# Moving every SBUF buffer of a fused attention and two-layer feed-forward kernel to a fixed place modulo 256 bytes

## The chip, the cores and the metric

The kernel runs on one core of one Trainium2 chip. The metric is the device time of one execution in microseconds, as a median over runs; beside it there is one execution taken with the hardware profiler, and all rows of a trace in this document come from such an execution. Every value is 32 bits wide, a tile has 128 partitions, and an address in this text is a byte offset within one partition of SBUF.

## The reference

Three blocks follow each other. The first is attention with random features, per batch (4) and head (8), sequence 576, head width 64, 128 features:

```python
q_p, k_p = phi(q * scale), phi(k * scale)    # phi: exp(x @ omega.T - |x|^2 / 2 - max) / sqrt(m)
kv = einsum('bhsm,bhsd->bhmd', k_p, v)
num = einsum('bhsm,bhmd->bhsd', q_p, kv)
den = einsum('bhsm,bhm->bhs', q_p, k_p.sum(axis=2)) + 1e-06
x = (num / den).transpose(0, 2, 1, 3).reshape(2304, 512)
```

The second (layer 1) is `(silu(x @ w_gate) * (x @ w_val)) @ w_out` with 1536 hidden columns, the third (layer 2) is `g(x @ w_in) @ w_out` with 2048 hidden columns, where `g` is 0 below -1, `(h + 1)^2 / 4` between -1 and 1, and `h` above 1.

## The kernel before, in words

**Order.** A planner in Python runs the whole kernel as a set of processes with priorities and a cost for each step, and thereby writes out by hand one fixed order of instructions for each engine. On the chip the engines run those orders and wait for each other through semaphores. A wait that ends late on the chip does not change the order.

**Products.** Nearly all work of TensorE is in `split3` (lines 398 to 400). Each operand is kept as a high and a low part in fp32r, and a product of two operands is three matmuls, high by high, high by low, low by high, each with a stationary operand of 128 columns and a moving operand of 256 columns:

```python
nc.tensor.matmul(ps, l_hi, r_hi, ...)   # L398: (accumulator, stationary, moving)
nc.tensor.matmul(ps, l_hi, r_lo, ...)   # L399
nc.tensor.matmul(ps, l_lo, r_hi, ...)   # L400
```

Each matmul has its own weight load, and the load for the next matmul runs while the present one streams. So the pair of addresses that are read together is the home of the next stationary operand and the home of the present moving operand.

**Stages.** Until about 257 us attention is computed, with the first part of layer 1 between its products. From 257 to about 601 us the rest of layer 1 follows, from there to the end layer 2. The late stages go through passes over four sets of weights in each layer (`passes`), in each over blocks of 512 tokens, with seven products for a 2 by 2 split of the block (`SEVEN`, `set_up`). In the order of TensorE the up products (x times the first weights) alternate with the down products (hidden rows times the second weights).

**Roles.** In the up products and in the down products of layer 1 (`out1`, `down1`) the weights are stationary, and what streams is x or the hidden row. In the down products of layer 2 (`down2`, `down_end`) the roles are turned: the hidden row is stationary and the weights stream. In attention the stationary operands are `ki`, `qi`, `ebk`, `ebq`, `xhl`, `kvz`, the moving ones `omr`, `omh`, `oml`, `vi`, `ids`, `qt`.

**Homes.** A ring is a list of free buffers of one role. The weights' slots are the rings' tiles `w` (9), `wx` (7, on the space of `lent` once attention's first block is done) and `wb` (8, on the space of `att` after attention, in the pool `rb`); x lives in `x1s` and `xur`, hidden rows in `hl` and `hlr`. Pools hand out addresses in the order of the code. The first 1,152 bytes are taken, so `pad0` of 352 bytes puts `w` at 1,504 + 4,096 i, which is 224 modulo 256; `pad1` of 160 puts `x1s` at 50,848, which is 160. With the other pads all of `w`, `wx`, `wb` are at 224 and all of `x1s`, `xur`, `hl`, `hlr` at 160. In attention `ebk`, `ebq`, `ki`, `vi`, `qi` and `xhl` are at 64, `qt`, `kvz` and `ids` at 192, `omr`, `omh`, `oml` at 224.

Of the kernel before, what the change touches and what calls it, by code (L numbers as in the profile page):

```python
# [42 lines left out]
SLACK_D, SLACK_U = 3.0, 0.8  # L43

SLACK_A = 0.0

NATK = 3

# [232 lines left out]
def performer_moe_kernel(ctx: ExitStack, tc: tile.TileContext, qG, kG, om, ident,  # L281
# [10 lines left out]
    def ring(*a):  # L292
        return Ring(bufs(*a))
# [4 lines left out]
    keep = ctx.enter_context(tc.tile_pool(name="keep", bufs=1, side="left"))  # L298
    acc = []
    bank = ring(psum, "bank", 8, [P, 512])  # L300
    def pad(pool, name, nbytes):
        pool.tile([P, nbytes // 4], F32, name=name)

    pad(keep, "pad0", 352)
    wring = ring(keep, "w", 9, [P, 2, 512], F32R)
    wstage = ring(keep, "ws", N_WS, [P, 1024], U32)
    wtmp = ring(keep, "wt", 2, [P, 512])
    half = keep.tile([P, 1], F32, name="half")
# [4 lines left out]
    x2q = [[dram.tile([P, KD, 512], F32, name=f"x2q{a}_{b}") for b in range(NBLK // 2 + 1)] for a in range(len(SETS1) - 1)]  # L313
    x2d = [dram.tile([P, 2, NBLK * TB], F32, name=f"x2d{d}") for d in range(2)]

    pad(keep, "pad1", 160)
    x1_sets = ring(keep, "x1s", 3, [P, 2, KD, TB], F32R)
    hbuf = ring(keep, "hb", 3, [P, 512])
    hrow = ring(keep, "hl", 2, [P, 2, 512], F32R)
    osb = ring(keep, "os", 3, [P, 512])  # L320
    xin = ring(keep, "xi", 2, [P, 512])
    xpart = ring(keep, "xp", 2, [P, 512])

    att_cm = tc.tile_pool(name="att", bufs=1, side="right", reuse_waits="tile")
    att = att_cm.__enter__()
    ebufs = {False: ring(att, "ebk", EBK, [P, 512]), True: ring(att, "ebq", EBQ, [P, 512])}
    kin = ring(att, "ki", KINS, [P, 512])
    vin = ring(att, "vi", VINS, [P, 576])
    qin = ring(att, "qi", QINS, [P, 512])
    lent_cm = tc.tile_pool(name="lent", bufs=1, side="left", reuse_waits="tile")  # L330
    lent = lent_cm.__enter__()
    lent_ids = set()
# [19 lines left out]
    lend(vin, "vl", N_VL, [P, 576])  # L352
    lend(qin, "ql", 2, [P, 512])
    lend(ebufs[False], "el", 2, [P, 512])
    nat_b = sorted({b for b in range(4) for k in range(NATK) if b * 576 < (k + 1) * TB and k * TB < (b + 1) * 576})
    kvr = {(b, d): att.tile([P, 2, 2, P], F32, name=f"kvr{b}_{d}") for b in nat_b for d in range(2)}
    qts0 = ring(att, "qtn", 3, [P, 2, TB])
    xhl = ring(att, "xhl", 2, [P, 2, 256], F32R)
    stat = ring(att, "st", 10, [P, 4, 4])
    rec = ring(att, "rec", 2, [P, TB])  # L360
    qts = ring(att, "qt", N_QT, [P, 2, 2, TB], F32R)
    kvz = [[att.tile([P, 2, 2, 2, P], F32R, name=f"kvz{b}_{d}") for d in range(2)] for b in range(2)]
    ids = att.tile([P, P], F32, name="ids")
    rect = ring(att, "rect", 1, [P, TB // 32, 33])
    nc.gpsimd.memset(rect.free[0][0][:, :, 32:33], 1e-6)
    omr = att.tile([P, 256], F32, name="omr")
    omh = att.tile([P, 256], F32R, name="omh")
    oml = att.tile([P, 256], F32R, name="oml")


    def dma(dst, src, nbytes):
# [52 lines left out]
        pl.put(wstage, st)  # L424
        return t

    def conv_key(key, src, slot):
        st = yield Get(wstage)
        pl.set(wdone[key])
        t = yield from to_f32(st, src, None)  # L430
        yield from parts(slot[:, 0], slot[:, 1], t, 512)
        pl.put(wtmp, t)
        wslot[key] = slot
        pl.set(wready[key])

    def conv(key, src, rng, prio):
# [2 lines left out]
        pl.spawn(conv_key(key, src, slot), prio)  # L439
        yield wdone[key]  # L440

    def wfree(key, rng):
        pl.put(rng, wslot.pop(key))

    moe_on = Ev()
    NE = N_EARLY[0]
# [55 lines left out]
    def w_feed():  # L502
        for m, a, order, sets in passes:
            for c in sets:
                for s, p in columns(m, c):
                    slots, tt = [], []
                    for i in range(2):
                        yield staged[s, 2 * p + i]
                    for _ in range(2):
                        tt.append((yield Get(wt2)))  # L510
                    for _ in range(4):
                        slots.append((yield Get(wring)))
                    pl.spawn(conv_pair(s, p, tt, slots), PR_W)
                for key in set_keys(m, c)[4:]:
                    yield staged[key]
                    t = yield Get(wt2)
                    slot = yield Get(wring)
                    pl.spawn(conv_one(key, t, slot), PR_W)

    def late_rank():  # L520
        return PR_C if moe_on.done else PR_CS
# [3 lines left out]
        wslot[key] = slot  # L525
        pl.set(wready[key])

    def conv_one(key, t, slot):
        yield from dma(t, w32[key], 262144)
        yield from conv_slot(key, t, slot)  # L530
        pl.put(wt2, t)

    def conv_pair(s, p, tt, slots):

        hs = [pl.spawn(dma(tt[i], w32[s, 2 * p + i], 262144), 0.6) for i in range(2)]
        for h in hs:
            yield h
        t0, t1 = tt
        lo, hi = slice(0, 256), slice(256, 512)
        yield from conv_slot((s, 2 * p), t0, slots[0])  # L540
        yield from conv_slot((s, 2 * p + 1), t1, slots[1])
        yield from two(t1[:, hi], t1[:, lo], t1[:, hi], 256, ALU.add)
        yield from two(t1[:, lo], t0[:, lo], t1[:, lo], 256, ALU.subtract)
        yield from two(t0[:, lo], t1[:, hi], t0[:, lo], 256, ALU.subtract)
        yield from two(t0[:, hi], t0[:, hi], t0[:, lo], 256, ALU.subtract)
        yield from conv_slot(("c" + s, p), t1, slots[2])
        pl.put(wt2, t1)
        yield from conv_slot(("d" + s, p), t0, slots[3])
        pl.put(wt2, t0)


# [376 lines left out]
    def att_close():  # L928
        for k in range(NBLK):
            yield x1_ready[k]  # L930
        att_cm.__exit__(None, None, None)
        rb = ctx.enter_context(tc.tile_pool(name="rb", bufs=1, side="right", reuse_waits="tile"))
        for rng, name, n, c in ((xpart, "xr", N_XR, [P, 512]), (ebr, "eb", N_EB, [P, 512]), (gbr, "gb", N_GB, [P, 1024]),
                                (wt2, "wtr", N_WT, [P, 512]), (hbuf, "hbr", N_HB, [P, 512]), (xq, "xq", N_XI, [P, 512])):
            for t in bufs(rb, name, n, c):
                pl.put(rng, t)
        for rng, name, n, more in ((hrow, "hlr", N_HL, 320), (wring, "wb", NB1, 192)):
            for t in bufs(rb, name, n, [P, 2, 512], F32R):
                pl.put(rng, t)
            pad(rb, "pad" + name, more)  # L940
        for t in bufs(rb, "xur", N_XU, [P, 2, 2, TB], F32R):
            pl.put(xu, t)
        pad(rb, "pad5", 320)
        pl.set(right_b)
        LEAN["DVE"], LEAN["POOL"] = LEAN_B, POOL_B

# [44 lines left out]
    def row_out(row, h):  # L991
        if len(row) > 2:
            if row[2] is not None:
                yield row[2]
        hl = yield Get(hrow)
        if len(row) > 2:
            pl.set(row[3])
        yield from parts(hl[:, 0], hl[:, 1], h, 512)
        pl.put(hbuf, h)
        row[1].append(hl)  # L1000
        pl.set(row[0])

    def evac1(k, d, last):
# [76 lines left out]
    def out1(step, h_ev, res):  # L1080
        k, fp = step
        first, last, end = run[step]
        for i in range(2):
            yield wready["o", 2 * fp + i]
        yield h_ev
        ws = [wslot["o", 2 * fp + i] for i in range(2)]
        hl = res[0]
        for n in range(KD):
            d, c = divmod(n, 2)
            if first and c == 0:  # L1090
                yield acc_free[d]
                acc_free[d] = Ev()
            for i in range(2):
                yield Op("PE", 3 * c_pe(TB), lambda: split3(
                    acc[d][:, c * TB:(c + 1) * TB], ws[i][:, 0, n * P:(n + 1) * P], ws[i][:, 1, n * P:(n + 1) * P],
                    hl[:, 0, i * TB:(i + 1) * TB], hl[:, 1, i * TB:(i + 1) * TB],
                    first and c == 0 and i == 0, last and i == 1, True))
            if last and c == 1:
                pl.spawn(evac1(k, d, end))
        pl.put(hrow, hl)  # L1100
        for f in (2 * fp, 2 * fp + 1):
            if last_use[f] == step:
                wfree(("o", f), wring)
# [155 lines left out]
    for m, a, order, sets in passes:  # L1259
        for j in order:  # L1260
            for c in sets:
                n = 2 if m == 1 and j < 4 else 1 if m == 1 else 4 if j < 4 else 2
                for r in range(n):
                    rows[m, a, j, c, r] = Ev(), [], before, Ev(), got, Ev()
                    before, got = rows[m, a, j, c, r][3], rows[m, a, j, c, r][5]

    def relu(dst, src, n):
# [310 lines left out]
    def late_down():  # L1578
        yield moe1_v
        yield from out1(*pend1.pop())  # L1580
        for m, a, order, sets in passes:
            for j in order:
# [14 lines left out]
                for i, (k, f, cols, end) in enumerate(todo):  # L1597
# [7 lines left out]
                    else:  # L1605
                        yield from (down1 if m == 1 else down2)(a, j, f, res[0], cols, i == 0, i == len(todo) - 1)
                    if end:
                        pl.put(hrow, res[0])
                    if j == order[-1]:
                        wfree(("o" if m == 1 else "p", f), wring)  # L1610

    def lent_close():
        yield x1_ready[0]
        lent_cm.__exit__(None, None, None)
        wl = ctx.enter_context(tc.tile_pool(name="wl", bufs=1, side="left", reuse_waits="tile"))
        pad(wl, "pad2", 320)
        for t in bufs(wl, "wx", NWL, [P, 2, 512], F32R):
            pl.put(wring, t)
        for t in bufs(wl, "wty", 2, [P, 512]):
            pl.put(wt2, t)  # L1620

# [98 lines left out]
```

## Time and profile before

| | |
|---|---|
| median of 3 runs | 973.72 us (971.79 to 978.3) |
| profiled execution | 974.34 us, its span 972.5 us |
| TensorE busy | 958.3 us of the span, 8,094 matmuls |
| VectorE / ScalarE / GpSimd busy | 825.9 / 567.4 / 96.4 us |
| DMA | 154.67 MB, mean 159 GB/s |

The span is the time from the first to the last instruction that the profiler saw; 1.8 us of the execution lie around it. A matmul's duration in the trace covers its way through the pipeline, so matmuls overlap, and the time from one start to the next is the pace. A window's count of matmuls includes the two or three that had begun before the window and were still in the pipeline.

### The profile page before, as it was taken

Reading aid. Unit: us, or ns where it says so; the run is one execution under the profiler, and the core shown is the slowest. Engines: PE = TensorE matmul, PEld = TensorE weight load, DVE = VectorE, ACT = ScalarE, POOL = GpSimd, SP = SyncE. Lnnn points to the kernel's source line nnn. Section 1 sums busy time; section 2 is a strip of 40 time slices with the busy share of each in tenths; the row PEclk is TensorE's granted clock in tenths of the full one; section 3 lists DMA queues with packets and bytes.
Section 4 is the critical chain, followed back from the end, with each engine's and each line's share of the span. In section 5 each row is a group of like instructions: output and inputs, shape, how many; then the busy total and the mean of one; then the engine's idle time right before and its main releaser. Section 6 shows DMA issues by size and latency. Waiting matters only on the chain.

```text
span 972.5 us, 21171 instructions
## 1 busy us (share of the span) xinstructions
PE 958.3 (99%) x8094; PEld 939.7 (97%) x8094; DVE 825.9 (85%) x1695; ACT 567.4 (58%) x1490; POOL 96.4 (10%) x99
## 2 busy tenths in 40 slices
PE   8999999999999999999999999999999999999998
PEld 6789999999999999999999999999999999999998
DVE  7999899888999999999999899899788768866553
ACT  8999788878645645445454566564445455544331
POOL 0332337434300000000000000000000000000000
PEclk9999999999999999999999999999999999999999
DMA  8766656635568465573657653445313041303022
GB/s 300 254 199 189 196 157 220 198 132 174 177 215 266 135 230 186 186 266 126 202 193 241 224 197 120 131 136 202 131 55 120 1 141 45 130 6 106 1 88 87
DMA packets 90677, 154.67 MB, mean 159 GB/s; under 512 B 8528, under 2 KB 42320, under 8 KB 90576
## 3 DMA queue, kind: packets, MB, share of 16 engines
q1 hardware_dynamic: 90576, 153.32, 48.2%
q8 instruction: 63, 1.03, 0.4%
q14 instruction: 38, 0.31, 0.1%
HBM read 110.30 MB, written 42.99 MB: 158 GB/s over the span
## 4 chain that ended last, share of the span: by engine, by line
PE 62%; DVE 11%; DMA 7%; ACT 4%; issue 2%; SPq 1%; POOL 0%; DVEq 0%; POOLq 0%; ACTq 0%
PE bank L398 20%; PE bank L400 20%; PE bank L399 20%; DMA ws<-in_wo_dram 2%; PE bank L875 2%; DMA ws<-in_w_dram 2%; DMA xq<-x1d 1%; DVE x1s L391 1%; DVE wt L422 1%; DVE wt L420 1%; DVE gb L1289 1%; DVE hb L1281 1%; DMA ki<-in_kG_dram 1%; PE bank L763 1%; PE bank L678 1%
## 5 line engine op out<-in xcount | busy, mean ns | idle before, releaser
L398 PE MATMUL bank<-x1s,w 128*128 128x256 f32 x492 | 139.0, 283 | 0.3 <-ACT eb L379 0.3
L400 PE MATMUL bank<-x1s,w 128*128 128x256 f32 x492 | 137.0, 278 | 0.0
L399 PE MATMUL bank<-x1s,w 128*128 128x256 f32 x492 | 136.9, 278 | 0.0
L398 PEld LDWEIGHTS bank<-x1s,w 128*128 128x128 f32 x492 | 92.8, 189 | 0.6 <-ACT eb L379 0.5
L400 PEld LDWEIGHTS bank<-x1s,w 128*128 128x128 f32 x492 | 92.6, 188 | 0.0
L399 PEld LDWEIGHTS bank<-x1s,w 128*128 128x128 f32 x492 | 92.5, 188 | 0.0
L379 ACT ACTIVATE x1s<-xq 128x512 fp32r<-128x512 f32 x81 | 50.8, 628 | 54.5 <-PE bank L400 35.0
L398 PE MATMUL bank<-x1s,wx 128*128 128x256 f32 x278 | 78.3, 282 | 2.3 <-ACT eb L379 1.8
L398 PE MATMUL bank<-x1s,wb 128*128 128x256 f32 x286 | 79.9, 279 | 0.0
L399 PE MATMUL bank<-x1s,wb 128*128 128x256 f32 x286 | 79.7, 279 | 0.0
L400 PE MATMUL bank<-x1s,wb 128*128 128x256 f32 x286 | 79.7, 279 | 0.0
L400 PE MATMUL bank<-x1s,wx 128*128 128x256 f32 x278 | 77.6, 279 | 0.0
L399 PE MATMUL bank<-x1s,wx 128*128 128x256 f32 x278 | 77.5, 279 | 0.0
L379 ACT ACTIVATE eb<-bank 128x512 f32<-128x512 f32 x95 | 56.1, 591 | 26.5 <-PE bank L400 26.0
L415 ACT ACTIVATE wt<-ws 128x512 f32<-128x512 f32 x68 | 45.9, 678 | 42.2 <-DMA ws<-in_w_dram 22.9
L391 DVE TENSOR_TENSOR x1s<-xq,x1s 128x512 fp32r<-128x512 f32 x90 | 61.7, 686 | 7.8 <-ACT x1s L379 7.4
L379 ACT ACTIVATE hlr<-hb 128x512 fp32r<-128x512 f32 x53 | 33.4, 631 | 52.7 <-PE bank L399 39.0
L398 PEld LDWEIGHTS bank<-x1s,wx 128*128 128x128 f32 x278 | 52.5, 189 | 3.3 <-ACT eb L379 2.6
L624 DVE TENSOR_REDUCE st<-bank 128x4 f32<-128x512 f32 x72 | 48.8, 684 | 7.7 <-PE bank L605 3.5
L1289 DVE TENSOR_TENSOR gb<-bank,eb 128x512 f32<-128x512 f32 x64 | 43.9, 686 | 12.3 <-PE bank L400 11.9
L398 PEld LDWEIGHTS bank<-x1s,wb 128*128 128x128 f32 x286 | 54.0, 189 | 0.2 <-DVE eb L1289 0.2
L400 PEld LDWEIGHTS bank<-x1s,wb 128*128 128x128 f32 x286 | 53.8, 188 | 0.0
(281 smaller groups left out, 3629.3 us busy)
## 6 DMA issues: line engine op xcount, KB each, us to landing
ws<-in_w_dram SPq DMA_DIRECT2D x40, 512.0 KB, 4.8
ws<-in_wo_dram SPq DMA_DIRECT2D x28, 512.0 KB, 5.3
xq<-x1d SPq DMA_DIRECT2D x36, 256.0 KB, 4.8
xq<-x2d SPq DMA_DIRECT2D x36, 256.0 KB, 3.9
qi<-in_qG_dram SPq DMA_DIRECT2D x34, 256.0 KB, 3.2
ki<-in_kG_dram SPq DMA_DIRECT2D x33, 256.0 KB, 3.5
vi<-in_kG_dram SPq DMA_DIRECT2D x28, 192.0 KB, 3.4
x1d<-os SPq DMA_DIRECT2D x18, 256.0 KB, 3.2
```

The costliest lines, as they stand in the source:

```text
L379: yield Op("ACT", c_act(n), lambda: nc.scalar.activation(dst, src, AF.Copy, scale=1.0 if scale is None else scale))
L391: yield Op("DVE", c_dve(n), lambda: nc.vector.tensor_tensor(out=dst, in0=a, in1=b, op=op), True)
L398: nc.tensor.matmul(ps, l_hi, r_hi, start=first, stop=False, skip_group_check=shared)
L399: nc.tensor.matmul(ps, l_hi, r_lo, start=False, stop=False, skip_group_check=shared)
L400: nc.tensor.matmul(ps, l_lo, r_hi, start=False, stop=last, skip_group_check=shared)
L415: yield Op("ACT", 0.575, lambda: nc.scalar.activation(t, hw.bitcast(F32), AF.Abs))
L420: yield Op("DVE", c_dve(512), lambda: nc.vector.scalar_tensor_tensor(out=ti, in0=lw, scalar=29, in1=ti, op0=ALU.logical_shift_right, op1=A ...
L422: yield Op("DVE", c_dve(512), lambda: nc.vector.scalar_tensor_tensor(out=ti, in0=hw, scalar=0xC0000000, in1=ti, op0=ALU.bitwise_and, op1=A ...
L624: yield Op("DVE", c_dve(512), lambda: nc.vector.tensor_reduce(out=st[:, :, 0], in_=psv, axis=AX.X, op=ALU.max, negate=True))
L678: nc.tensor.matmul(kp[:, 2 * pr + a], e[:, u * P:(u + 1) * P], vb[:, vi + (dv if li == 4 else 0), a * 64:a * 64 + P], start=(li == 0 and a ...
L875: nc.tensor.matmul(ps[:, a, c0:c1], kz[:, l, r, a], q_t[:, h, a, c0:c1], start=(l == 0 and h == 0), stop=(l == 1), skip_group_check=True)
L1289: yield Op("DVE", c_dve(512), lambda: nc.vector.tensor_tensor(out=dst, in0=pq(ps), in1=pq(e), op=ALU.add))
```

## The change

No instruction is added, taken away or reordered by the code; the planner's costs and priorities are the same. Three things move.

First, the order of the tiles in the pools `keep`, `att` and `rb` and the pads between them. Second, a slot for weights is 4,352 bytes in place of 4,096 (1,088 columns), and a process chooses where in the slot its 1,024 columns begin: at 0 for the weights of up products and of the down products of layer 1 (`O_OFF`), 48 columns or 192 bytes further for the weights of layer 2's down products (`P_OFF`). Third, the hidden rows of a pool are views of one tile, 1,024 columns apart and 1,072 long, and a row of layer 2 begins 16 columns or 64 bytes further (`H_OFF`).

Counted through as above, the weights of up products and of layer 1's down products stay at 224 modulo 256, those of layer 2's down products come to 160, x and the rows of layer 1 stay at 160, and the rows of layer 2 come to 224. In attention all stationary operands come to 224 and all moving ones to 160. So for every matmul after which a load follows, inside a group and where one kind of product follows another, the next stationary operand lies 64 bytes modulo 256 behind the present moving one. Before, the difference was:

| pair (next stationary, present moving) | before | after |
|---|---|---|
| up products; layer 1's down products; the steps between them | 64 | 64 |
| layer 2's down products | 192 | 64 |
| from up to down and from down to up in layer 2 | 0 | 64 |
| `kvz` with `qt` | 0 | 64 |
| `xhl` with `omh`, `oml`; `ki` with `omr` | 96 | 64 |
| `ebk` with `vi`; `ebq` with `ids` | 0; 128 | 64; 64 |

```diff
+O_OFF, P_OFF, H_OFF = 0, 48, 16
...
+    def split_at(t, off):
+        return t[:, off:off + 1024].rearrange("p (h c) -> p h c", h=2)
...
-    pad(keep, "pad0", 352)
-    wring = ring(keep, "w", 9, [P, 2, 512], F32R)
+    wring, hrow = Ring([]), Ring([])
+    def slot_tiles(pool, name, n):
+        for t in bufs(pool, name, n, [P, 1088], F32R):
+            pl.put(wring, t)
+    def row_tiles(pool, name, n):
+        t = pool.tile([P, 1024 * n + 48], F32R, name=name)
+        for i in range(n):
+            v = t[:, 1024 * i:1024 * i + 1072]
+            pl.put(hrow, v)
+    pad(keep, "pad0", 32)
+    x1_sets = ring(keep, "x1s", 3, [P, 2, KD, TB], F32R)
+    row_tiles(keep, "hl", 2)
...
-    pad(keep, "pad1", 160)
-    x1_sets = ring(keep, "x1s", 3, [P, 2, KD, TB], F32R)
-    hrow = ring(keep, "hl", 2, [P, 2, 512], F32R)
+    pad(keep, "pad1", 96)
+    slot_tiles(keep, "w", 9)
...
     att = att_cm.__enter__()
+    stat = ring(att, "st", 10, [P, 4, 4])
+    rec = ring(att, "rec", 2, [P, TB])
+    rect = ring(att, "rect", 1, [P, TB // 32, 33])
+    vin = ring(att, "vi", VINS, [P, 576])
+    qts0 = ring(att, "qtn", 3, [P, 2, TB])
+    qts = ring(att, "qt", N_QT, [P, 2, 2, TB], F32R)
+    ids = att.tile([P, P], F32, name="ids")
+    omr = att.tile([P, 256], F32, name="omr")
...
+    pad(att, "pada", 64)
     ebufs = {False: ring(att, "ebk", EBK, [P, 512]), True: ring(att, "ebq", EBQ, [P, 512])}
     kin = ring(att, "ki", KINS, [P, 512])
-    vin = ring(att, "vi", VINS, [P, 576])
     qin = ring(att, "qi", QINS, [P, 512])
...
+    xhl = ring(att, "xhl", 2, [P, 2, 256], F32R)
+    kvz = [[att.tile([P, 2, 2, 2, P], F32R, name=f"kvz{b}_{d}") for d in range(2)] for b in range(2)]
...
-        yield from conv_slot(key, t, slot)
+        yield from conv_slot(key, t, split_at(raw, O_OFF if key[0] == "o" else P_OFF))
...
-        for rng, name, n, more in ((hrow, "hlr", N_HL, 320), (wring, "wb", NB1, 192)):
-            for t in bufs(rb, name, n, [P, 2, 512], F32R):
-                pl.put(rng, t)
-            pad(rb, "pad" + name, more)
-        for t in bufs(rb, "xur", N_XU, [P, 2, 2, TB], F32R):
+        row_tiles(rb, "hlr", N_HL)
+        pad(rb, "padj", 64)
+        xur = bufs(rb, "xur", N_XU, [P, 2, 2, TB], F32R)
+        pad(rb, "padk", 64)
+        slot_tiles(rb, "wb", NB1)
+        for t in xur:
             pl.put(xu, t)
...
-        hl = yield Get(hrow)
+        raw = yield Get(hrow)
+        hl = split_at(raw, H_OFF if len(row) > 2 and row[6] == 2 else 0)
...
-        pad(wl, "pad2", 320)
-        for t in bufs(wl, "wx", NWL, [P, 2, 512], F32R):
-            pl.put(wring, t)
+        slot_tiles(wl, "wx", NWL)
```

The rest of the diff hands the whole slot or row (`raw`, `whole`) back to its ring in place of the view.

## Rows read from the trace of the kernel before

**Rows 1.** The page: span, busy time of each engine, and granted clock by slices.

```profile
span 972.5 us, 21171 instructions
...
PE 958.3 (99%) x8094; PEld 939.7 (97%) x8094; DVE 825.9 (85%) x1695; ACT 567.4 (58%) x1490; POOL 96.4 (10%) x99
...
PEclk9999999999999999999999999999999999999999
```

**Rows 2.** Windows without a wait: busy us (instructions), granted clock, DMA share, GB/s.

```profile
core 0: us, PE busy (x) PEld busy (x) DVE busy (x) ACT busy (x) POOL busy (x), PEclk, DMA share, GB/s
...
258.00:304.00 46.00, 46.00 (x408) 46.00 (x408) 42.70 (x78) 21.84 (x40) 3.52 (x3) 1.00 0.68 221
...
430.00:490.00 60.00, 60.00 (x512) 60.00 (x511) 58.18 (x114) 32.24 (x62) 0.00 (x0) 1.00 0.56 184
498.00:520.00 22.00, 22.00 (x197) 22.00 (x196) 20.33 (x38) 8.03 (x16) 0.00 (x0) 1.00 0.47 146
526.00:553.00 27.00, 27.00 (x240) 27.00 (x240) 24.16 (x47) 11.66 (x23) 0.00 (x0) 1.00 0.55 180
560.00:600.00 40.00, 40.00 (x342) 40.00 (x341) 39.85 (x76) 25.41 (x47) 0.00 (x0) 1.00 0.54 178
605.00:945.00 340.00, 340.00 (x2932) 340.00 (x2931) 259.76 (x458) 161.11 (x290) 0.00 (x0) 1.00 0.29 93
776.00:790.00 14.00, 14.00 (x126) 14.00 (x125) 8.21 (x16) 8.42 (x16) 0.00 (x0) 1.00 0.49 170
946.00:970.00 24.00, 22.83 (x202) 22.63 (x200) 9.97 (x16) 4.21 (x7) 0.00 (x0) 1.00 0.24 77
```

**Rows 3.** Timeline of TensorE in layer 2: first matmul of five groups of six.

```profile
640.68 0.28 PE L398 MATMUL bank<-x1s,w 128*128 128x256 f32 x1
...
641.37 0.28 PE L398 MATMUL bank<-w,hl 128*128 128x256 f32 x1
...
642.05 0.28 PE L398 MATMUL bank<-x1s,w 128*128 128x256 f32 x1
...
642.76 0.28 PE L398 MATMUL bank<-w,hl 128*128 128x256 f32 x1
...
643.47 0.28 PE L398 MATMUL bank<-x1s,wx 128*128 128x256 f32 x1
```

**Rows 4.** Timeline of TensorE: the matmuls that followed three waits in layer 1.

```profile
493.76 0.39 PE L398 MATMUL bank<-x1s,wx 128*128 128x256 f32 x1 [0.86 <-ACT eb L379]
...
524.34 0.38 PE L398 MATMUL bank<-x1s,wx 128*128 128x256 f32 x1 [0.38 <-ACT eb L379]
...
554.73 0.39 PE L398 MATMUL bank<-x1s,wx 128*128 128x256 f32 x1 [0.18 <-ACT eb L379]
```

**Rows 5.** Waits of TensorE from 555 us to the end.

```profile
PE bank L398 <- ACT eb L379: 0.2, 1, 0.2
```

**Rows 6.** Timeline of TensorE (the first row) and its groups by line, attention.

```profile
254.77 1.60 PE L875 MATMUL bank<-qt,kvz 128*128 128x256 f32 x12
...
L399 PE MATMUL bank<-oml,xhl 128*128 128x256 f32 x58 | 16.3, 281 | 0.0
...
L875 PE MATMUL bank<-qt,kvz 128*128 128x256 f32 x96 | 13.5, 283 | 0.0
```

**Rows 7.** First use of `xq` by DMA and last use of `qt` by TensorE.

```profile
L372 SPq DMA_DIRECT2D xq<-x1d x36: 360/426/1341, 266.4 to 540.0; - x36
...
L875 PE MATMUL bank<-qt,kvz x192: 216/280/365, 113.5 to 256.1; 128*128 128x256 f32 x96, 128*128 128x128 f32 x48, 128*128 128x192 f32 x24, 128*128 128x64 f32 x24
```

**Rows 8.** Timeline: ScalarE writes a unit of `x1s`, TensorE streams `x1s`.

```profile
523.19 0.62 ACT L379 ACTIVATE x1s<-xq 128x512 fp32r<-128x512 f32 x1
...
523.46 0.28 PE L398 MATMUL bank<-x1s,wb 128*128 128x256 f32 x1
```

More of the change, by code (lines that the diff above doesn't have):

```diff
@@ L322, in performer_moe_kernel @@
     xpart = ring(keep, "xp", 2, [P, 512])
+    pad(keep, "pad1", 96)
+    slot_tiles(keep, "w", 9)
     att_cm = tc.tile_pool(name="att", bufs=1, side="right", reuse_waits="tile")
     att = att_cm.__enter__()
+    stat = ring(att, "st", 10, [P, 4, 4])
[6 more added lines that the diff above has]
+    omr = att.tile([P, 256], F32, name="omr")
+    omh = att.tile([P, 256], F32R, name="omh")
+    oml = att.tile([P, 256], F32R, name="oml")
+    pad(att, "pada", 64)
     ebufs = {False: ring(att, "ebk", EBK, [P, 512]), True: ring(att, "ebq", EBQ, [P, 512])}
     kin = ring(att, "ki", KINS, [P, 512])
-    vin = ring(att, "vi", VINS, [P, 576])
     qin = ring(att, "qi", QINS, [P, 512])
+    nat_b = sorted({b for b in range(4) for k in range(NATK) if b * 576 < (k + 1) * TB and k * TB < (b + 1) * 576})
+    kvr = {(b, d): att.tile([P, 2, 2, P], F32, name=f"kvr{b}_{d}") for b in nat_b for d in range(2)}
+    xhl = ring(att, "xhl", 2, [P, 2, 256], F32R)
+    kvz = [[att.tile([P, 2, 2, 2, P], F32R, name=f"kvz{b}_{d}") for d in range(2)] for b in range(2)]
     lent_cm = tc.tile_pool(name="lent", bufs=1, side="left", reuse_waits="tile")
@@ L354, in performer_moe_kernel @@
     lend(ebufs[False], "el", 2, [P, 512])
[L355 to L364, printed above, removed]
     nc.gpsimd.memset(rect.free[0][0][:, :, 32:33], 1e-6)
-    omr = att.tile([P, 256], F32, name="omr")
-    omh = att.tile([P, 256], F32R, name="omh")
-    oml = att.tile([P, 256], F32R, name="oml")
     def dma(dst, src, nbytes):
@@ L425, in to_f32, with conv_key @@
         return t
-    def conv_key(key, src, slot):
+    def conv_key(key, src, raw):
+        whole[key] = raw
+        slot = split_at(raw, 0)
         st = yield Get(wstage)
@@ L440, in conv @@
         yield wdone[key]
+    whole = {}
     def wfree(key, rng):
-        pl.put(rng, wslot.pop(key))
+        del wslot[key]
+        pl.put(rng, whole.pop(key))
     moe_on = Ev()
@@ L516, in w_feed @@
                     t = yield Get(wt2)
-                    slot = yield Get(wring)
-                    pl.spawn(conv_one(key, t, slot), PR_W)
+                    raw = yield Get(wring)
+                    pl.spawn(conv_one(key, t, raw), PR_W)
     def late_rank():
@@ L526, in conv_slot, with conv_one, up @@
         pl.set(wready[key])
-    def conv_one(key, t, slot):
+    def conv_one(key, t, raw):
         yield from dma(t, w32[key], 262144)
-        yield from conv_slot(key, t, slot)
+        yield from conv_slot(key, t, split_at(raw, O_OFF if key[0] == "o" else P_OFF))
+        whole[key] = raw
         pl.put(wt2, t)
     def conv_pair(s, p, tt, slots):
+        def up(key, t, raw):
+            whole[key] = raw
+            return conv_slot(key, t, split_at(raw, 0))
         hs = [pl.spawn(dma(tt[i], w32[s, 2 * p + i], 262144), 0.6) for i in range(2)]
@@ L539, in conv_pair @@
         lo, hi = slice(0, 256), slice(256, 512)
-        yield from conv_slot((s, 2 * p), t0, slots[0])
-        yield from conv_slot((s, 2 * p + 1), t1, slots[1])
+        yield from up((s, 2 * p), t0, slots[0])
+        yield from up((s, 2 * p + 1), t1, slots[1])
         yield from two(t1[:, hi], t1[:, lo], t1[:, hi], 256, ALU.add)
@@ L545, in conv_pair @@
         yield from two(t0[:, hi], t0[:, hi], t0[:, lo], 256, ALU.subtract)
-        yield from conv_slot(("c" + s, p), t1, slots[2])
+        yield from up(("c" + s, p), t1, slots[2])
         pl.put(wt2, t1)
-        yield from conv_slot(("d" + s, p), t0, slots[3])
+        yield from up(("d" + s, p), t0, slots[3])
         pl.put(wt2, t0)
@@ L936, in att_close @@
                 pl.put(rng, t)
-        for rng, name, n, more in ((hrow, "hlr", N_HL, 320), (wring, "wb", NB1, 192)):
-            for t in bufs(rb, name, n, [P, 2, 512], F32R):
-                pl.put(rng, t)
-            pad(rb, "pad" + name, more)
-        for t in bufs(rb, "xur", N_XU, [P, 2, 2, TB], F32R):
+        row_tiles(rb, "hlr", N_HL)
[4 more added lines that the diff above has]
+        for t in xur:
             pl.put(xu, t)
-        pad(rb, "pad5", 320)
         pl.set(right_b)
@@ L1000, in row_out @@
         row[1].append(hl)
+        row[1].append(raw)
         pl.set(row[0])
@@ L1099, in out1 @@
                 pl.spawn(evac1(k, d, end))
-        pl.put(hrow, hl)
+        pl.put(hrow, res[1])
         for f in (2 * fp, 2 * fp + 1):
@@ L1263, in performer_moe_kernel @@
                 for r in range(n):
-                    rows[m, a, j, c, r] = Ev(), [], before, Ev(), got, Ev()
+                    rows[m, a, j, c, r] = Ev(), [], before, Ev(), got, Ev(), m
                     before, got = rows[m, a, j, c, r][3], rows[m, a, j, c, r][5]
@@ L1607, in late_down @@
                     if end:
-                        pl.put(hrow, res[0])
+                        pl.put(hrow, res[1])
                     if j == order[-1]:
```

## The prediction

> **What bounds the kernel now.** I read the page first: TensorE is busy for 99% of the span and VectorE for 85%, and the granted clock is full in every slice [rows 1]. So the end is set by the sum of the times from one matmul to the next, and the clock gives nothing back. The change touches no instruction; it can act only on this pace or on waits.
>
> The second view is the busy time in windows in which TensorE never waits [rows 2]. There the window divided by the number of matmuls is the pace. From each count I take 2.4 off, the matmuls still in the pipeline at the window's start (0.28 us each at some 0.116 us). In 258 to 304 us that is 46.00 / 405.6 = 113.4 ns; 498 to 520, 526 to 553 and 776 to 790 give 113 to 114 as well. In 430 to 490 it is 60.00 / 509.6 = 117.7 and in 560 to 600 117.8. All are full matmuls of 256 columns, granted clock 1.00. So the same work has two paces, **fast** (113.4) and **slow** (117.8), 4.4 ns or 3.9% apart, and each holds for tens of microseconds. Both occur in layer 1, where the difference of addresses is 64 throughout.
>
> Layer 2 is neither: 605 to 945 us has 340.00 / 2929.6 = 116.1 ns. The timeline shows why [rows 3]. From 641.37 to 642.05, six matmuls of a down product, 0.68 us (113); from 642.05 to 642.76, an up product, 0.71 (118); the next down product again 0.71 (118). In the up product before, 640.68 to 641.37, it is 0.69, since its first interval is long and the rest fast. Through this stretch the pace turns over at each step from down to up, where the difference is 0, and stays at the step from up to down, which is 0 too; down products alone, in which the difference is 192, hold a pace (776 to 790 us, fast).
>
> The third view is the waits. What sets the pace in layer 1 is the restart after a wait: after the one before 493.76 the pace is fast, after 524.34 fast, after 554.73 slow [rows 2, 4]. There are ten such stops from 300 to 560 us, three of them shown; counted by the starts that follow, six went on fast and four slow. After 554.73, whose wait is the one in [rows 5], TensorE has not one more.
>
> **The change, part by part.** All terms are made against the profiled execution, 974.3 us (972.5 of span and 1.8 around it), which is 0.6 above the median.
>
> *Layer 2, steps at 0.* The steps from down to up and from up to down come to 64, as in layer 1, where such steps neither turn the pace over nor cost a longer interval. So layer 2 should behave like layer 1: the pace drawn at the last wait holds. If fast, 605 to 945 us gives 2929.6 x (116.1 - 113.4) = 7.9 us back. If slow, it costs 2929.6 x (117.8 - 116.1) = 5.0, and 946 to 970, fast now with some 200 matmuls [rows 2], costs 200 x 4.4 = 0.9 more: 5.8 together. With six draws in ten fast: 0.6 x (-7.9) + 0.4 x 5.8 = -2.4 us. I take this value since one run need not be one draw. At a fast pace TensorE arrives up to 8 us earlier, and each new wait is a new draw.
>
> *Layer 2's down products, 192 to 64.* At 192 both paces occur, at 64 too: nothing, bounded by the two values above, which include these matmuls.
>
> *Layer 1 after attention.* No difference changes. The slow stretches, 419 to 494 and 555 to 601 us, are 121 of the 344 us from 257 to 601. The draws are made anew: 121 x 4.4 / 117.8 = 4.5 us less if all fast, 223 x 4.4 / 113.4 = 8.7 more if all slow. With four in ten slow in place of 35% it is no change; I take 0.
>
> *Attention.* `qt` with `kvz` lies at 0 and goes at (1.60 - 0.28) / 11 = 120 ns [rows 6]; there are 96 such matmuls of full width, and 3 x 58 with `xhl`, which I price at the same 120 as an upper bound. Made fast, 270 x 6.6 = 1.8 us; made slow, 270 x 2.2 = 0.6. I take 1.2. The float32 products (`ki`, `vi`, `ids`) change their differences as well, and no row tells their pace at another one; I leave them at 0 and take the 1.8 of the nearest priced group as a bound to either side.
>
> *What costs nothing.* The pools' new order puts other tiles on the space that attention leaves. The four `xq` come to lie on `qt`, `ids` and `omr`, which are used last; but the first load into `xq` is issued at 266.4 us and the last product on `qt` starts at 256.1 [rows 7], so the cover is 10 us; if it were gone, that load and what SyncE has behind it, the next loads and stores of the same queue, would be later, and the first up products after attention with them. The rows of a pool become views of one tile. Waits could now tie both rows together, and a row would then be written only when its neighbour has been read. In `x1s` two units share one tile already, and ScalarE writes a unit from 523.19 to 523.81 while TensorE streams the other, at 523.46 for one [rows 8]: so waits go by region, and I price this at 0. Where layer 2's first row, shifted by 64 bytes, reaches into the end of its neighbour of layer 1, one wait is true; it happens once per pool. DMA moves the same bytes in the same runs, at a start that was no multiple of 256 before and is none after.
>
> Sum: 974.3 - 1.2 - 2.4 = 970.7 for the profiled execution, 970 against the median of the runs.
>
> **A rule against the change.** Rows 2 show two paces for the same matmul and rows 3 show them turn over from one group to the next. The Trainium skill, SBUF — State Buffer, section "SBUF: two separate sides", says that among the engines only the port pair that VectorE shares with GpSimd causes contention, and that PE never waits on anyone; TensorE: Matmul & The Clock Gate, "Step-by-step: what each phase is for", adds that loading the next tile's weights takes no SBUF read bandwidth from the running matmul. By that, addresses could not matter, and the sum would be 0. The paces at 0 difference (120 ns with `kvz`, and the turnovers) speak against it, though they don't prove that the address is the cause.
>
> **The rivals.**
>
> *Fast throughout.* If 64 in every pair keeps the two reads from meeting, also after a restart, all stretches run at 113.4: 974.3 - 7.9 - 4.5 - 1.8 = 960, 959.5 against the median. For it: the longest stretches at 64 are fast. Against it: 430 to 490 and 560 to 600 us are at 64 in all pairs and slow [rows 2]. Waits of TensorE would be added, since VectorE is busy for 39.85 of 40 us in 560 to 600.
>
> *Slow held to the end.* This ends on the other side. In 560 to 600 VectorE has no room [rows 2]. A fast TensorE there runs into waits, each a draw, until it draws slow; a slow one does not wait and keeps its pace, because from 605 us on VectorE is busy for only 260 of 340 us. What now frees layer 2 from a slow start, the turnover at 0, is gone. Price: 974.3 - 0.6 + 5.8 = 979.5, 979 against the median, and up to 987 if layer 1 draws slow too. It decides from the point where more than 7.9 / 13.7 = 58% of layer 2 is slow; from there the second layer is a loss.
>
> *No effect.* If the pace hangs on something else than the address (a count of matmuls, the writes of other engines), layer 2 goes on alternating: 974.
>
> **How the numbers follow.** The forecast, pace held in layer 2 and mixed over a run or over the runs: 0.5, 970 us, own range 964 to 978. Fast throughout: 0.24, 958 to 963. Slow held: 0.18, 977 to 987. No effect: 0.08, 972 to 976. A measurement of this kernel tells about 1% from no change, that is 964 and 983.5. Faster takes all of the second case and a little of the first: 0.25. Slower takes the upper part of the third: 0.05. The rest is 0.70. The range from 960 to 981 leaves out some 0.1 of the fast case and 0.06 of the slow one.
>
> **What would show it.** In the changed trace 605 to 945 us (some microseconds earlier or later) has a pace of 113.4 or 117.8, or both in long stretches with a wait between; groups of six no longer alternate. If they still do, the difference of 0 is not what turns the pace. If `qt` with `kvz` stays at 120, the term of attention falls. If slow stretches at 64 are gone everywhere, the draw after a wait was an effect of something else and the fast rival holds. The prediction is wrong by a cost that I left at zero if TensorE shows new waits at 257 to 300 us, or before the down products of layer 2 on rows of `hl` or `hlr`.

## The result, and the profile after

In 14 runs each, the changed kernel has a median of 979.08 us (961.6 to 981.9) and the kernel before 976.3 (970.94 to 981.42); the means are 975.8 and 976.0. The single times say more than either:

```
changed   961.60 962.39 968.55 969.91 | 978.25 978.72 978.89 979.26 979.35 980.17 980.30 980.43 981.17 981.90
```

Four runs lie at 961 to 970 us and ten at 978 to 982, with nothing between. The ratio that goes with these runs, 0.9894 with a 95% interval of 0.9851 to 0.9936, leaves out runs more than 1.5% above a kernel's fastest, and with that the ten; here they are no disturbance but the more frequent outcome of the kernel, at the same granted clock (0.998 to 1.000 in both groups), so I read all 14. The profiled execution is one of the ten: 980.3 us, span 978.5.

The page of the changed kernel answers to [rows 1]:

```profile
span 978.5 us, 21166 instructions
...
PE 962.4 (98%) x8094; PEld 943.5 (96%) x8094; DVE 826.4 (84%) x1695; ACT 567.5 (58%) x1490; POOL 96.8 (10%) x99
...
PEclk9999999999999999999999999999999999999999
```

The same matmuls, the same work on the other engines, the clock granted in full, and 6.0 us more. The windows, which answer to [rows 2], show where:

```profile
328.00:416.00 88.00, 88.00 (x779) 88.00 (x778) 84.44 (x164) 43.09 (x80) 0.00 (x0) 1.00 0.56 182
...
560.00:592.00 32.00, 32.00 (x284) 32.00 (x284) 31.72 (x61) 20.48 (x37) 0.00 (x0) 1.00 0.54 180
605.00:945.00 340.00, 340.00 (x2889) 340.00 (x2889) 259.25 (x457) 158.82 (x288) 0.00 (x0) 1.00 0.28 93
```

With 2.4 taken off each count as in the prediction, 560 to 592 us is 32.00 / 281.6 = 113.6 ns per matmul, fast. 605 to 945 us is 340.00 / 2886.6 = 117.8, slow over its whole length. Before it was 116.1 there. The timeline in layer 2, which answers to [rows 3], has no turnover left:

```profile
641.11 0.28 PE L416 MATMUL bank<-x1s,w 128*128 128x256 f32 x1
...
641.82 0.28 PE L416 MATMUL bank<-w,hl 128*128 128x256 f32 x1
...
642.52 0.28 PE L416 MATMUL bank<-x1s,w 128*128 128x256 f32 x1
...
643.23 0.28 PE L416 MATMUL bank<-w,hl 128*128 128x256 f32 x1
```

Groups of six take 0.71, 0.70 and 0.71 us: up and down products alike are slow, with no longer interval at the steps. The draw that decided this is in the timeline a little before 605 us:

```profile
593.93 0.28 PE L416 MATMUL bank<-hl,w 128*128 128x256 f32 x1
594.04 0.28 PE L417 MATMUL bank<-hl,w 128*128 128x256 f32 x1
594.15 0.28 PE L418 MATMUL bank<-hl,w 128*128 128x256 f32 x1
594.37 0.38 PE L416 MATMUL bank<-x1s,wb 128*128 128x256 f32 x1
594.59 0.28 PE L417 MATMUL bank<-x1s,wb 128*128 128x256 f32 x1
594.71 0.28 PE L418 MATMUL bank<-x1s,wb 128*128 128x256 f32 x1
594.82 0.28 PE L416 MATMUL bank<-x1s,wb 128*128 128x256 f32 x1
594.94 0.28 PE L417 MATMUL bank<-x1s,wb 128*128 128x256 f32 x1
```

Up to 594.15 a matmul starts every 0.11 us; then 0.22 pass, a stop so short that the view of waits does not list it; after the restart the starts are 0.12 apart, and they stay so to the end of the kernel.

The stages of the profiled executions, read from the starts of the last product on `qt`, of layer 2's first down product and of the last matmul, add up the same way. "Pace" is the mean interval of the full matmuls, intervals over 128 ns left out, and "stops" is what those took beyond 113.3 ns:

| | attention ends | layer 1: time, pace, stops | layer 2: time, pace |
|---|---|---|---|
| before | 256.1 us | 351.7 us, 115.0 ns, 7.4 us | 360.7 us, 115.9 ns |
| changed | 257.4 | 350.5, 114.4, 8.0 | 366.6, 117.8 |

Layer 2 has no stop in either. Its 5.9 us are the whole difference of the spans: attention ends 1.3 us later and layer 1 is shorter by as much.

### The profile page after: what moved, and what is told of

The parts are those of the page before. It is cut to its first block, busy times and chain, and to the rows that moved or that the text cites. A ratio compares the mean times of both kernels' runs of the same rounds, so it can differ in the third digit from the quotient of the medians.

```text
span 978.5 us, 21166 instructions
## 1 busy us (share of the span) xinstructions
PE 962.4 (98%) x8094; PEld 943.5 (96%) x8094; DVE 826.4 (84%) x1695; ACT 567.5 (58%) x1490; POOL 96.8 (10%) x99
## 4 chain that ended last, share of the span: by engine, by line
PE 77%; DMA 8%; DVE 7%; ACT 6%; issue 2%; SPq 1%; POOL 0%; DVEq 0%; ACTq 0%; POOLq 0%
PE bank L416 23%; PE bank L417 23%; PE bank L418 23%; PE bank L705 2%; PE bank L632 2%; DMA ws<-in_w_dram 2%; DMA ws<-in_wo_dram 2%; PE bank L902 2%; PE bank L790 1%; DMA ki<-in_kG_dram 1%; DMA xq<-x1d 1%; PE bank L894 1%; ACT ki L605 1%; ACT ebq L659 1%; DVE wt L438 1%
```

## The experiments

The theory is that the difference of addresses decides which paces exist and that a step at another difference moves the pace, while at 64 it holds. The rivals are that the slow layer 2 comes from something else in the new layout, and that only waits change the pace. In the first four kernels the changed kernel has other offsets; `U_OFF` is added for the weights of up products.

**Layer 2 as it was.** `-O_OFF, P_OFF, H_OFF = 0, 48, 16` `+U_OFF, O_OFF, P_OFF, H_OFF = 0, 0, 0, 0`

> The changed kernel with H_OFF and P_OFF at 0: layer 2 has again a difference of 192 inside its down products and 0 at the steps between up and down; attention and everything else stay as changed. If the steps at 0 turn the pace over (my theory), layer 2 alternates again, 605 to 945 us at 116.1 ns per matmul, and all runs lie together within 970 to 978 us: no cluster at 978 to 982 and none at 960 to 965. If the slow second layer of the changed kernel comes from something else in the new layout (the longer slots, the rows in one tile, other homes of what DMA and VectorE touch), it stays at 117.8 ns and about 979 us.

Measured: 974.65 us median, 12 runs, 969.96 to 977.9, one cluster; ratio to before 1.0002 (0.998 to 1.0024). Its windows:

```profile
605.00:945.00 340.00, 340.00 (x2931) 340.00 (x2931) 259.84 (x458) 160.83 (x290) 0.00 (x0) 1.00 0.28 93
946.00:956.00 10.00, 10.00 (x90) 10.00 (x90) 4.66 (x7) 3.79 (x6) 0.00 (x0) 1.00 0.01 2
```

340.00 / 2928.6 = 116.1 ns, the alternating pace of before; layer 2 takes 360.7 us again. So the two clusters come from layer 2's differences alone. All else in the layout, attention's homes included, shows no effect; the interval leaves room for some 2 us either way.

**128, 192 and 0 in every pair of both layers.** `+U_OFF, O_OFF, P_OFF, H_OFF = 16, 16, 48, 32` for 128; `32, 32, 48, 48` for 192; `48, 48, 48, 0` for 0.

> The changed kernel with a difference of 128 in place of 64 in every pair of both layers, the steps included; attention's own pairs stay at 64. No row shows 128 for these matmuls yet. My theory says that the difference decides what paces exist: either two paces that hold as at 64 and 192 (then the runs fall into two clusters, some 960 to 970 and 977 to 982 us), or one (then they lie together: 958 to 963 if fast, 981 to 988 if slow). If the address has no part in it, the runs look like those of the changed kernel.

> The changed kernel with a difference of 192 in every pair of both layers, the steps included. In the kernel before, layer 2's down products at 192 kept a fast pace (776 to 790 us) and a slow one (642.76 to 643.35). My theory: two paces, both of which hold, the one drawn at a wait; runs in two clusters as in the changed kernel. If 192 has only one stable pace, the runs lie together, at 958 to 963 or at 981 to 988 us.

> The changed kernel with a difference of 0 in every pair of both layers. Before the change, kvz with qt at 0 went at a steady 120 ns. My theory: about 6,090 matmuls after 257 us at 120 ns in place of about 115.9, some 25 us more than the kernel before less the waits that disappear: 992 to 1003 us, all runs together. If the address has no part in it: 979 us, as the changed kernel.

Measured: 128 has 990.01 us median (989.24 to 991.52, 6 runs, ratio 1.0166, 1.014 to 1.0191); 192 has 982.63 (981.2 to 985.32, 6 runs, 1.0093, 1.0069 to 1.0117); 0 has 997.02 (996.19 to 998.71, 5 runs, 1.0237, 1.0212 to 1.0263). One or two windows of each, in this order:

```profile
605.00:945.00 340.00, 340.00 (x2868) 340.00 (x2867) 259.97 (x458) 162.28 (x293) 0.00 (x0) 1.00 0.28 90
```

```profile
258.00:304.00 46.00, 46.00 (x408) 46.00 (x407) 43.10 (x79) 21.99 (x40) 3.51 (x3) 1.00 0.68 225
...
605.00:945.00 340.00, 340.00 (x2890) 340.00 (x2889) 260.41 (x461) 161.41 (x292) 0.00 (x0) 1.00 0.28 93
```

```profile
258.00:304.00 46.00, 46.00 (x386) 46.00 (x385) 42.07 (x78) 22.06 (x39) 4.03 (x3) 1.00 0.67 213
...
605.00:945.00 340.00, 340.00 (x2835) 340.00 (x2835) 259.11 (x457) 162.96 (x295) 0.00 (x0) 1.00 0.27 89
```

From 605 to 945 us the counts give 118.6, 117.7 and 120.0 ns. The rival of no effect is out: these offsets alone move the median from 974.65 us (layer 2 as it was) to 997.02. At 0 and at 128 there is one pace, and the runs lie together, for 0 where I expected them, for 128 above the 981 to 988 that I gave a slow kernel, since its pace is a third one. At 192 the trace has the fast pace too (256 to 304 us, 113.3 ns), but after the stop at 305 us it is slow to the end, through seven more restarts, counted by the starts, and no run is below 981: the two paces exist, as I expected; a second cluster did not show in six runs, which do not rule it out.

**Other steps around down products at 64.** Inside all products 64; in layer 2 the steps from up to down and from down to up are 96 and 32 (`P_OFF, H_OFF = 56, 24`), 32 and 96 (`40, 8`), 128 and 0 (`0, 32`), 0 and 128 (`32, 0`).

> As the changed kernel, 64 inside all products, but in layer 2 the step from up to down has a difference of 96 and the step from down to up 32 (H_OFF 24, P_OFF 56). If a step's difference can change the pace that the groups then keep (my theory, from the steps at 0 which turn it over), layer 2 gets a pace of its own that does not depend on the draw at the last wait: fast after every step gives 605 to 945 us at 113 to 114 ns and runs at 962 to 970 us, alternating gives 116 ns and 970 to 978 us, in either case one cluster. If only waits change the pace, the runs fall into the two clusters of the changed kernel, most of them at 977 to 982 us.

> The same with 32 from up to down and 96 from down to up (H_OFF 8, P_OFF 40). Same readings: one cluster, at 962 to 970 us if the steps lead to the fast pace, 970 to 978 us if they turn it over, above 981 us if they lead to the slow one and cost longer intervals; two clusters, most runs at 977 to 982 us, if only waits change the pace.

> The same with 128 from up to down and 0 from down to up (H_OFF 32, P_OFF 0). The step at 0 from down to up is the one that turned the pace over before the change; if that alone does it, layer 2 alternates again unless 128 changes the pace too: one cluster at 970 to 978 us. Two clusters, most runs at 977 to 982 us, if only waits change the pace.

> The same with 0 from up to down and 128 from down to up (H_OFF 0, P_OFF 32). The step at 0 from up to down left the pace alone before the change; a steady 128 in all pairs gave 118.7 ns. If 128 at a step leads to the slow pace, one cluster at 980 to 985 us; if it turns the pace over, 970 to 978 us; if it leads to the fast pace, 962 to 970 us; two clusters if only waits change the pace.

| steps | median, range of 12 runs | ratio (interval) | layer 2: time, pace |
|---|---|---|---|
| 96, 32 | 978.72 (974.51 to 983.36) | 1.0041 (1.0016 to 1.0066) | 364.7 us, 117.2 ns |
| 32, 96 | 979.31 (977.34 to 981.7) | 1.0054 (1.0027 to 1.008) | 366.2, 117.6 |
| 128, 0 | 977.6 (974.12 to 979.27) | 1.0033 (1.0012 to 1.0055) | 364.8, 117.2 |
| 0, 128 | 975.68 (973.41 to 979.91) | 1.0021 (0.9996 to 1.0046) | 363.3, 116.7 |

Each is one cluster. For the first two that alone would also fit a slow draw in every run; the traces decide, and in them the steps, not the last draw, set layer 2's pace. In all four a step of 0 or 96 leads from slow to fast within the next group and costs longer intervals on the way, and a step of 32 or 128 leads back. With 96 and 32 the timeline has

```profile
652.19 0.28 PE L416 MATMUL bank<-x1s,wb 128*128 128x256 f32 x1
...
652.90 0.28 PE L416 MATMUL bank<-wx,hlr 128*128 128x256 f32 x1
653.02 0.29 PE L417 MATMUL bank<-wx,hlr 128*128 128x256 f32 x1
653.14 0.28 PE L418 MATMUL bank<-wx,hlr 128*128 128x256 f32 x1
653.26 0.28 PE L416 MATMUL bank<-wx,hlr 128*128 128x256 f32 x1
653.37 0.28 PE L417 MATMUL bank<-wx,hlr 128*128 128x256 f32 x1
...
653.60 0.28 PE L416 MATMUL bank<-x1s,wx 128*128 128x256 f32 x1
```

The up product is slow (0.71 us for six); the down product begins with starts 0.12 apart, becomes fast at 653.26, and the next up product is slow again. None of these leads to a lasting fast pace, and the times of layer 2 lie between those of an alternating and a slow one (360.7 and 366.6 us): the longer intervals cost most of what the groups at the fast pace bring. This cost is not in the 970 to 978 us that I gave an alternating layer 2, and the first two medians lie above it.

**A probe of steps.** To find a step after which the pace is fast, one more matmul stands before each bank that layer 2's up products open:

```diff
+    STEPS = [(p, q) for p in (0, 64, 128, 192) for q in (0, 64, 128, 192)]
+    def extra(ps, raw, x):
+        here, there = STEPS[n_extra[0] * 5 % 16]
+        n_extra[0] += 1
+        s0, m0 = (here - 64) // 4 % 64, (64 - there) // 4 % 64
+        nc.tensor.matmul(ps[:, 0:256], raw[:, s0:s0 + P],
+                         x[:, 0].rearrange("p k c -> p (k c)")[:, m0:m0 + 256], start=True, stop=False, ...)
```

> The changed kernel (64 in all pairs) with one matmul more before each of the 48 accumulator banks that layer 2's up products open; the product's first matmul overwrites what it wrote, so it serves only as a step. Its own weights lie p bytes behind what streams before it, and the product's first weights lie q bytes behind what it streams; p and q go through the 16 pairs of 0, 64, 128, 192, three times each. My theory: a step off 64 moves the pace, so the pace of layer 2 changes at some of the 48 places and only there, always in the same way for the same pair and the same pace before; 64 with 64 changes nothing. The useful find would be a pair after which the pace is fast whatever it was before. Rival: only waits draw the pace; then layer 2 keeps one pace over all 48 places. The extra matmuls cost 48 x 0.115 = 5.5 us in either case.

One run, 976.17 us. The pace before each of the 48 places and the pace on which it settled some six to eight matmuls after it, from the starts (F fast, S slow), p down and q across:

```
p \ q   0              64             128            192
0       F>S S>F S>F    F>S F>S F>S    F>F F>F F>F    F>F F>F F>F
64      S>S S>S S>S    S>S F>F F>F    S>F S>F S>F    F>S F>S F>S
128     F>F F>F F>F    S>F S>F S>F    S>F F>F F>F    F>S F>S F>S
192     S>F S>F S>F    F>F F>F F>F    F>F F>F F>F    F>S F>S F>S
```

No pair led the same pace to two different ones. 64 with 64 changes nothing; 0 with 0 turns the pace over. 128 with 128 is the one pair seen to lead to fast from both sides, once from slow and twice from fast. The starts around its first place, at 586.13:

```profile
585.77 0.28 PE L416 MATMUL bank<-hlr,w 128*128 128x256 f32 x1
585.89 0.28 PE L417 MATMUL bank<-hlr,w 128*128 128x256 f32 x1
586.01 0.28 PE L418 MATMUL bank<-hlr,w 128*128 128x256 f32 x1
586.13 0.28 PE L1420 MATMUL bank<-x1s,wb 128*128 128x256 f32 x1
586.25 0.28 PE L416 MATMUL bank<-x1s,wb 128*128 128x256 f32 x1
...
586.95 0.28 PE L416 MATMUL bank<-hlr,w 128*128 128x256 f32 x1
...
587.29 0.28 PE L416 MATMUL bank<-hlr,w 128*128 128x256 f32 x1
...
587.63 0.28 PE L416 MATMUL bank<-x1s,wx 128*128 128x256 f32 x1
```

Six matmuls take 0.70 us up to 586.95, and the six after it 0.68, three of them 0.34: fast.

**The step put to use, and two controls.** The probe's matmul with 128 and 128 alone, once at the first up product of each block in layer 2's two passes, eight in all; the same eight with 64 and 64; and the first with eight more in layer 1.

```diff
+                    if m == 2 and first and i == 0 and bk == "U" and c in {sets[0] for _, _, _, sets in passes}:
+                        extra(ps, whole[wk1], x)
```

> The changed kernel with one matmul more at the first up product of each block in layer 2's two passes (8 in all), whose result the next matmul overwrites, with differences 128 into it and 128 out of it. In the probe a fast pace followed on this pair each time, from a slow pace as from a fast one. If steps of addresses set the pace, layer 2 runs at 113.4 to 114 ns nearly throughout, at most with a slow stretch up to the next of the eight places, and takes 353 to 356 us instead of 366.6; all runs together at 964 to 970 us, without the cluster at 977 to 982. If the probe's runs were chance, two clusters as in the changed kernel.

> The same eight extra matmuls with differences 64 and 64. If it is the step of addresses that brings back the fast pace, these change nothing but 8 x 0.115 = 0.9 us: runs in the two clusters of the changed kernel, most at 978 to 983 us. If any extra matmul would do, it is as fast as the kernel with 128 and 128.

> The kernel with 128 and 128, with eight more such matmuls at the same places of layer 1's passes (16 in all). In the kernels so far layer 1 after attention took 350 to 355 us at any pace from 113.4 to 117.1 ns, since TensorE waited for more when it was faster. If VectorE sets the time of layer 1, this brings nothing: layer 1 350 to 353 us, the runs within 2 us of those with eight. If TensorE sets it, layer 1 shortens to some 345 us and the runs by about as much.

| | median, range | ratio (interval) | layer 1: time, pace, stops | layer 2: time, pace |
|---|---|---|---|---|
| 128 in layer 2 | 964.15 (962.03 to 970.24), 6 runs | 0.9914 (0.9885 to 0.9943) | 349.5 us, 114.3 ns, 7.1 us | 353.8 us, 113.4 ns |
| 64 in layer 2 | 967.32 (963.69 to 982.8), 12 runs | 0.9928 (0.9913 to 0.9942), of the nine runs below 971 | 351.2, 115.5, 5.2 | 353.6, 113.3 |
| 128 in both | 967.62 (966.11 to 969.52), 6 runs | 0.994 (0.9923 to 0.9957) | 350.5, 113.5, 9.5 | 354.0, 113.5 |

The kernel before had 973.75 us beside these. With 128 all twelve runs of the two kernels are below 970.3 us. With 64 nine runs are at 963.7 to 970.1 and three at 980.1 to 982.8: two clusters, as expected, though most runs are in the lower one and not in the upper. Twelve of twelve against nine of twelve may be chance, so these times do not show by themselves that the step repairs a slow draw. Nor does the trace of the kernel with 128 in layer 2: its eight extra matmuls, by the starts, all found the fast pace, and its time shows what a fast layer 2 is worth. The profiled execution of the control is one of the nine and shows layer 2 at a fast pace with nothing that brings it back:

```profile
605.00:945.00 340.00, 340.00 (x3002) 340.00 (x3001) 263.61 (x466) 163.60 (x294) 0.00 (x0) 1.00 0.29 93
```

340.00 / 2999.6 = 113.4 ns, layer 2 13.0 us shorter than in the changed kernel's trace. In the kernel with 128 in both layers, the trace does have a slow draw and its repair, beside the probe the one place where this step met a slow pace. At 603.46 TensorE restarts after a stop of some 50 ns, and slow starts follow; the extra matmul stands at 611.28, and from 612.11 six take 0.68 us again:

```profile
603.35 0.28 PE L418 MATMUL bank<-hl,w 128*128 128x256 f32 x1
603.46 0.33 PE L416 MATMUL bank<-xur,wx 128*128 128x256 f32 x1
603.63 0.28 PE L417 MATMUL bank<-xur,wx 128*128 128x256 f32 x1
...
611.28 0.28 PE L1415 MATMUL bank<-x1s,wb 128*128 128x256 f32 x1
...
612.11 0.28 PE L416 MATMUL bank<-wb,hlr 128*128 128x256 f32 x1
...
612.79 0.28 PE L416 MATMUL bank<-x1s,wx 128*128 128x256 f32 x1
```

Layer 1 gains nothing from its eight, as I expected if VectorE sets its time: the pace falls from 114.3 to 113.5 ns and the stops rise from 7.1 to 9.5 us. The median is 3.5 us above that with eight in layer 2, not within the 2 I gave; this has no explanation.

## Why the prediction was right, and where it was not

**The mechanism** was right. Layer 2 stopped alternating, kept the pace of its last draw, and layer 2 as it was (first experiment) brought the alternation back. The sizes were right too: the slow price of 5.8 us was 5.9, and the fast gain of 7.9 was 360.7 - 353.6 = 7.1, or 8.0 without the control's eight extra matmuls of 0.113 (the control's trace stands in, since none of the changed kernel's four times at 961 to 970 us was profiled).

**The forecast's value** was not. The step that failed is in the term of layer 2: six draws in ten fast, and from that a mean of -2.4 us. Four runs in 14 were fast. The six in ten came from a count of all restarts in layer 1, and that is the wrong count: in the changed trace ten of the twelve restarts of layer 1 went on fast, counted by the starts, and the last one did not. And since this one draw near 600 us decides nearly the whole stage, a run is one draw; 970 us was the mean of two outcomes, two runs came within 2 us of it and ten at 978 to 982. The value of the likeliest case should have been that of one outcome. That the median of 979.08 us lies in the range of 960 to 981 owes more to the width of the range, which holds most of both outcomes, than to the forecast, whose own range ended at 978. The rival "slow held to the end", to which I gave 0.18, came with 979 us in ten runs of 14. Its reason was the trace's: VectorE is busy for 31.72 of 32 us in 560 to 592, a fast TensorE was stopped until 594.37, and the draw was slow. How often it is slow I cannot tell from the experiments: with eight idle extra matmuls three runs of 12 were slow in place of ten of 14. That the moment of the restart decides is likely but was only argued, and whether chance, the extra matmuls, the place or the chip made this difference stays open.

**Attention** was priced at 1.2 us and brought nothing that shows: with attention's new homes and the old layer 2 the ratio is 1.0002, but its interval (0.998 to 1.0024) is too wide to refute 1.2 us. The pace of `qt` with `kvz` did move as forecast, twelve matmuls in 1.53 us in the changed trace against 1.60 [rows 6], but 96 of them are 0.6 us at most.

```profile
250.42 1.53 PE L902 MATMUL bank<-qt,kvz 128*128 128x256 f32 x12
```

**Layer 1** was left at 0 for the wrong reason, equal draws. In the eleven traces with layer 1's own pairs at 64 it takes 349.5 to 354.5 us at paces from 113.4 to 115.5 ns, and is no shorter where the pace is faster: the stops grow in its place (5.2 us at 115.5 ns, 13.0 at 113.4) and give it all back. TensorE then waits for more than one engine. In the trace with 128 in both layers the first two rows of its waits after 257 us (total us, times, longest) are

```profile
PE bank L416 <- ACT eb L397: 3.3, 4, 1.9
PE bank L416 <- DVE eb L1318: 2.4, 2, 1.8
```

that is, for `eb` written by ScalarE or by VectorE. That VectorE, busy for nearly all of such windows, sets the time of the stage is likely but not shown. Where TensorE is slower the pace counts: at 120.0 ns layer 1 took 360.3 us, with 1.0 us of stops.

**The terms at nothing** held: TensorE's waits for hidden rows after attention are 1.3 us in the changed trace against 1.6 before, so none for a neighbour in the same tile shows, and layer 2 has no stop at all. **The rule** that TensorE never waits on anyone at SBUF (the Trainium skill, SBUF — State Buffer, section "SBUF: two separate sides") leaves no room for what was measured: with the same instructions the difference of addresses alone makes the pace 120.0 ns (0), 118.6 (128), or one of 113.4 and 117.8 (64). What in the chip holds a matmul up, no row shows.

## What to carry to other kernels

Where TensorE runs back to back with a weight load beside each matmul, take the pace of each stage from a window without waits; if it is not one number, look at the addresses modulo 256 of what is read together. A layout in which two paces both hold is a lottery, and its mean may be no better than that of a layout that alternates; ask what draws the pace, and whether one step can be placed that leads to the good one from both. Put it only in the stages that TensorE sets: here the kernel with eight such matmuls in layer 2 ran in 964.15 us, 9.6 below the kernel before beside it, and eight more in layer 1 brought nothing. How much of the 9.6 the step itself earned is not shown, since eight matmuls that change no difference gave a fast layer 2 in nine runs of 12; what is shown is that the step ended a slow pace in two traces, once in each, and that no run of 12 with it was slow.

## What the runs showed of the hardware

Four differences give, for fp32r matmuls of 256 columns with 128 columns of weights, at the full granted clock: 0 modulo 256 a steady 120.0 ns, 128 a steady 118.6, 64 and 192 either 113.3 or 117.8. It is the difference and not the place, as far as two places tell: 0 gave 120 with both reads at 192 (`kvz` with `qt`, before) and with both at 160 (0 in every pair). And the pace is a state that outlives what set it: once entered at 64 it held for up to 366 us and some 3,100 matmuls, through all changes of operands and of engines' work beside it, and after attention it ended only at a stop of TensorE or at a step of another difference. A stop of some 50 ns changed it once (603.46 us, above).
